# Unread TensorE products at seven value sums of an attention kernel with a feed-forward block

## The chip, the cores and the metric

The kernel runs on one core of a Trainium2 chip. The metric is the device time of one execution in microseconds (us). The engines are named as in the profile: PE is TensorE, PEld its weight loads, DVE VectorE, ACT ScalarE, POOL GpSimd, SP SyncE, whose queue issues the DMAs.

## The reference

Inputs q, k, v of shape (8 batches, 8 heads, 576 positions, 64), w_in (512 x 2048) and w_out (2048 x 512), all float32.

```python
scores = scale * np.matmul(q, k.transpose(0, 1, 3, 2))
kth = np.partition(scores, -top_k, axis=-1)[..., -top_k:-top_k + 1]   # top_k = 32
scores = np.where(scores >= kth, scores, -1000000000.0)
attn = np.exp(scores - np.max(scores, axis=-1, keepdims=True))
attn = attn / (np.sum(attn, axis=-1, keepdims=True) + 1e-09)
x = np.matmul(attn, v)            # heads are then set side by side: (4608, 512)
h = x @ w_in
out = (h - np.tanh(h)) @ w_out    # (4608, 512)
```

## The kernel before, in words

The attention is cut into 144 steps. A step is one pair of heads and 128 query rows (or the last 64 rows of two pairs of heads, a "rem" step). Its stages lie in successive iterations of one loop (`run`), so that several steps are under way at once:

- `scores` (L238): PE multiplies q and k into PSUM, ACT copies the result out (L246).
- `search` (L268 to L279): DVE finds the 32nd largest score of each row by rounds of MAX8 and MATCH_REPLACE8.
- `mask` (L295 to L315): POOL makes the threshold `tb`, ACT (L308) and POOL (L311) put everything below it out, POOL writes a check (`bad`, L315).
- `expo` (L331): ACT takes the exponentials, with the sum of each row. POOL adds epsilon to the sums (L341), DVE inverts them (L346), and POOL repeats each inverse 64 times into the tile `rx` (L356, `spread`): the "repeated sums" of the change.
- Turning. The exponentials have to stand with the keys on the partitions. In the steps of batch 0 (`pe` steps, the ones that the change touches) PE does that: `turn_pe` makes nine transposes (L412) into three PSUM tiles `zt` of four, four and one, and ACT copies each out into `et` (L415). In the other steps DVE and DMAs do it (`turn_z`, `spread_keys`).
- `values` (L436, L444, L448, L460): ten PE products (five chunks of keys, two heads) sum the values into `av[:, 0]`, a transpose of `rx` (L444) sets the repeated sums beside them in `av[:, 1]`, ACT copies both out as `xs` (L448), and POOL multiplies the two (L460) into `xT`, the input of the feed-forward block.
- `ffn_h` (L489, with tanh and the difference at L501 to L503) and `ffn_o` (L510, L520) are the feed-forward block, cut into items of 8 matmul calls or of 2 (L510). `deal` places them between the stages, as many as `rate` asks for; they begin after step 3, which ends the first block of 128 rows.

In a `pe` step n the order in which PE's instructions are written is, in iteration n+2: eight transposes (two `zt` tiles), the scores of step n+3, the ninth transpose (the third `zt` tile), feed-forward items if there are any, then `values(n)`. ACT's order in the same iteration is: two copies of `zt` (L415), L308 of the step after, the conversion of the weights (below), the copy of the scores (L246), the third copy of `zt` (L415), the exponentials of the step after (L331), the tanh of an item, and the copy `xs` (L448). Each engine works its own list in order.

`values(n)` is called only for the last step of a group of rows. In batch 0 the first two blocks of 128 rows have groups of one step (steps 0 to 7); then two steps make a group (8 and 9, and so on).

The pool `zt_ps` has two PSUM buffers; `zt` tiles and `av` tiles share the tag "zt" and with it these two buffers. A tile that takes a buffer waits for the last reader of the tile that had it.

In the first some 160 us the weights are also converted (`convert`, L148 to L173): DMAs bring 32 pieces, and DVE, ACT and POOL work on each. The scheduler follows the program order (`manual_schedule`), and the framework sets the waits.

Of the kernel before, what the change touches and what calls it, by code (L numbers as in the profile page):

```python
# [10 lines left out]
FP32 = mybir.dt.float32  # L11
# [37 lines left out]
def kernel(  # L49
# [9 lines left out]
    nc = tc.nc  # L59
    P = nc.NUM_PARTITIONS  # L60
# [22 lines left out]
    def pool(name, bufs, **kw):  # L83
        return ctx.enter_context(tc.tile_pool(name=name, bufs=bufs, **kw))
# [15 lines left out]
    zt_ps = pool("zt_ps", 2, space=PS)  # L100
    h_ps = pool("h_ps", 2, space=PS)

    ident = consts.tile([P, P], FP32, name="ident")
# [80 lines left out]
    def half(t):  # L184
        return slice(t * D, (t + 1) * D)
# [179 lines left out]
    def tiles(x, nq):  # L365

        x = x[:, 0 : nq * 2 * S]
        return x.rearrange("p (a k i j) -> p a k i j", a=NG, k=KC, j=G)
# [28 lines left out]
    def turn_pe(n):  # L397
# [10 lines left out]
        for k0 in range(0, KC, J):  # L408
# [10 lines left out]
            if k0:  # L419
                yield  # L420

    def values(n):

        g = steps[n]
        nq, u = g.nq, g.unit
        et = tiles(ets.pop(n), nq)
        rx = rxs.pop(n)
        w = nq * P
        av = zt_ps.tile([P, 2, N], FP32, tag="zt", name="av")
        for i in range(2 if g.rem else 1):  # L430
            cols = half(i) if g.rem else slice(0, w)
            es = et[:, 2 * i : 2 * i + 2] if g.rem else et
            hp = g.hp + i
            for c in range(J + 1):
                for t in range(2):
                    nc.tensor.matmul(  # L436
                        av[half(t), 0, cols],
                        vb[g.b, hp][:, t, c, :] if c < J else vr[g.b, hp][:, t, :],
                        es[:, :, (J + 1) * t + c if c < J else J].rearrange("p a i j -> p a (i j)"),
                        start=(c == 0),  # L440
                        stop=(c == J),
                    )
        for i in range(nq):
            nc.tensor.transpose(  # L444
                av[:, 1, 0:w].rearrange("p (a i j) -> p i a j", a=NG, i=nq)[:, i], rx[:, i].rearrange("p t d -> p (t d)"), ident[:]
            )
        xs = xrpool.tile([P, 2, N], FP32, tag="xs", name="xs")
        nc.scalar.copy(xs[:, :, 0:w], av[:, :, 0:w])  # L448
        if g.rem:
            for i in range(2):  # L450
                nc.gpsimd.tensor_tensor(
                    xt(u)[:, g.hp + i, g.col : g.col + R],
                    xs[:, 0, half(i)],
                    xs[:, 1, half(i)],
                    ALU.mult,
                )
        else:

            xv = xs[:, :, 0:w].rearrange("p s (a i j) -> p s i a j", a=NG, i=nq)
            nc.gpsimd.tensor_tensor(  # L460
                xt(u)[:, g.hp, g.col : g.col + w].rearrange("p (i a j) -> p i a j", a=NG, i=nq),
                xv[:, 0],
                xv[:, 1],
                ALU.mult,
            )
        if n in done:
            work.extend(ffn(u))
# [3 lines left out]
    def xt(u):  # L471
        if u.xT is None:
            p = xpool if u.tag == "xT" else xrpool
            u.xT = p.tile([P, CD, N], FP32, tag=u.tag, name=u.tag)
        return u.xT
# [48 lines left out]
    def ffn(u):  # L524

        nh = CF * u.n // (2 * P)
        for item in range(nh):
            f = (item + 1) * CF // nh - 1
            yield CD * (f // FJ + 1), u, lambda item=item: ffn_h(u, item)
        for i in range(len(u.blocks)):  # L530
            for part in range(CF // 2):
                yield CD * (WJ + part // 2 + 1), None, lambda i=i, part=part: ffn_o(u, i, part)

    steps, done, work = [], {}, []

    def plan():
        steps.clear(), done.clear()

        def block(b, qt):
            return [(slice(0, P), out[b * S + qt * P : b * S + (qt + 1) * P, :])]

        rest = None
        for b in range(B):
            if b % 2 == 0:
                rest = Unit(
                    [[(half(i), out[(b + i) * S + JP : (b + i + 1) * S, :]) for i in range(2)]], "xTr"
                )

            parts = [(0, 1), (2, 3)]
            if b == 0:
                parts[0:1] = [(0,), (1,)]
            for a, qts in enumerate(parts):
                unit = Unit([block(b, qt) for qt in qts], "xT")
                pe = b == 0
                for hp in range(NHP):
                    for i, qt in enumerate(qts):
                        steps.append(Step(b, hp, qt, unit, 0, i, len(qts), pe))
                    if hp == NHP - 1:  # L560
                        done[len(steps) - 1] = unit
                    if hp % 2 and a == (0 if b == B - 1 else len(parts) - 1):
                        steps.append(Step(b, hp - 1, J, rest, b % 2 * R, pe=pe))
                        if hp == NHP - 1 and b % 2:
                            done[len(steps) - 1] = rest
        for g, after in zip(steps, steps[1:]):
            if after.pe and not after.rem and not g.pe:
                g.lag = 3
# [4 lines left out]
    def run(exact):  # L573
# [119 lines left out]
        for n in range(-4, NS + 4):  # L693
# [3 lines left out]
            for m in (n - 4, n - 3):  # L697
                if 0 <= m < NS and steps[m].last and steps[m].lag == n - m:
                    values(m)
# [22 lines left out]
            if pe and steps[n - 2].last:  # L722
                values(n - 2)
# [52 lines left out]
```

## Time and profile before

| what | value |
|---|---|
| median of 4 runs | 1539.3 us (1537.58 to 1540.37) |
| profiled execution | 1538.49 us, its span 1536.7 us |
| PE busy | 1439.6 us, 94% of the span |
| PEld busy | 910.0 us, 59% |
| DVE busy | 1347.0 us, 88% |
| POOL busy | 940.9 us, 61% |
| ACT busy | 883.4 us, 57% |
| mean granted clock of PE | 0.98 |

The span goes from the first to the last instruction that the profiler records; the time of the execution is 1.8 us longer. The granted clock is the share of full speed that PE was given in a stretch of time. Busy shares are means over the whole span; the early part, in which the weights are converted, looks different from the rest. In a list of instructions in order of time each line gives the start, the duration, the engine, the line of the kernel, the operation, the tiles (out<-in), the shape, the number of records, and in brackets how long the engine was idle before it and what ended that. One float32 matmul call leaves two MATMUL records, a transpose one.

### The profile page before, as it was taken

The page shows a single profiled execution, that of the slowest core. Times are in us where ns is not written, and L with a number is a line of the kernel's source. Part 1 is how long each engine was busy: PE and PEld are TensorE (multiplying, and loading weights), DVE is VectorE, ACT ScalarE, POOL GpSimd, SP SyncE. Part 2 cuts the span into 40 slices and gives each one's busy share as a digit, 9 for nine tenths or more (in the row PEclk, how much of TensorE's full clock was granted, in tenths as well). Part 3 has the DMA queues.
Part 4 walks back from the last instruction along what each step waited for, and adds up shares of the span by engine and source line. Part 5 has one row for each costly group of instructions (what it writes and reads, how often), then busy time and mean ns, then how long its engine had stood idle before and what let it go on. Part 6 is the DMA issues. An engine that isn't in the chain of part 4 may idle for free.

```text
span 1536.7 us, 24174 instructions
## 1 busy us (share of the span) xinstructions
PE 1439.6 (94%) x7428; PEld 910.0 (59%) x7428; DVE 1347.0 (88%) x3828; ACT 883.4 (57%) x1567; POOL 940.9 (61%) x1525
## 2 busy tenths in 40 slices
PE   2567898999999999999999999999999999999997
PEld 1355566565666666656566665656566665656673
DVE  7997999999999999999999999999999999997300
ACT  4887776566555555555555565556565565655320
POOL 3777576567666665656575675757575675746420
PEclk9787999999999999999999999999999999999999
DMA  9954214547755575446754575446655566534400
GB/s 250 363 182 146 50 32 108 138 142 175 183 142 145 139 174 155 130 138 153 184 139 138 146 172 159 128 141 155 177 136 147 145 154 164 146 115 116 138 7 16
DMA packets 255466, 221.61 MB, mean 144 GB/s; under 512 B 197728, under 2 KB 204896, under 8 KB 248160
## 3 DMA queue, kind: packets, MB, share of 16 engines
q1 hardware_dynamic: 253552, 219.75, 53.0%
q8 instruction: 61, 1.00, 0.3%
q14 instruction: 77, 0.63, 0.1%
q10 hardware_dynamic: 1776, 0.22, 0.1%
HBM read 136.17 MB, written 83.76 MB: 143 GB/s over the span
## 4 chain that ended last, share of the span: by engine, by line
PE 77%; DVE 9%; ACT 4%; DMA 4%; POOL 2%; SPq 2%; issue 2%; DVEq 0%; ACTq 0%; POOLq 0%
PE hps L489 30%; PE ops L510 27%; PE av L436 10%; PE scps L238 9%; DVE m L276 2%; DVE ab L279 2%; PE av L444 2%; SPq L201 1%; DMA et<-there 1%; DMA zx<-in_moe_w_in_dram 1%; ACT z L308 1%; PE zt L412 1%; POOL z L311 1%; DMA there<-spare 1%; DVE ab L268 1%
## 5 line engine op out<-in xcount | busy, mean ns | idle before, releaser
L510 PE MATMUL ops<-w_out,g 128*128 128x512 f32 x1152 | 520.3, 598 | 0.0
L276 DVE MAX8 m<-ab 128x8 f32<-128x288 f32 (+1 forms) x1152 | 471.5, 457 | 0.0
L489 PE MATMUL hps<-xT,w_in 128*128 128x256 f32 (+1 forms) x2176 | 470.1, 371 | 1.2 <-POOL xT L460 1.2
L311 POOL TENSOR_TENSOR z<-sc,z 128x576 f32<-128x576 f32 x288 | 400.2, 1411 | 75.3 <-ACT z L308 75.3
L489 PEld LDWEIGHTS hps<-xT,w_in 128*128 128x128 f32 x2176 | 389.6, 192 | 73.9 <-issue 21.8
L279 DVE MATCH_REPLACE8 ab<-m,ab 128x288 f32<-128x288 f32 x864 | 381.5, 456 | 0.0
L510 PEld LDWEIGHTS ops<-w_out,g 128*128 128x128 f32 x1152 | 211.3, 191 | 244.6 <-issue 240.5
L308 ACT ACTIVATE z<-sc,tb 128x576 f32<-128x576 f32 x288 | 207.6, 769 | 153.4 <-POOL tb L295 153.4
L503 POOL TENSOR_TENSOR g<-g,th 128x512 f32<-128x512 f32 x144 | 183.7, 1276 | 123.4 <-ACT g L502 106.6
L331 ACT ACTIVATE z<-z,nb 128x576 f32<-128x576 f32 x288 | 221.6, 773 | 8.8 <-POOL z L311 8.7
L246 ACT COPY sc<-scps 128x1152 f32<-128x1152 f32 x144 | 160.8, 1117 | 108.8 <-PE scps L238 106.6
L238 PE MATMUL scps<-kT,qT 64*128 64x288 f32 (+1 forms) x1280 | 188.1, 445 | 29.7 <-DVE qT L223 27.3
L238 PEld LDWEIGHTS scps<-kT,qT 64*128 64x128 f32 (+1 forms) x1280 | 101.5, 184 | 118.5 <-issue 55.9
L436 PE MATMUL av<-et,vb 128*64 128x256 f32 (+1 forms) x1088 | 132.9, 380 | 39.0 <-ACT et L415 31.4
L268 DVE TENSOR_TENSOR ab<-scps,sc 128x576 f32<-128x576 f32 x144 | 108.9, 757 | 68.0 <-POOL bad L315 56.2
L460 POOL TENSOR_TENSOR xT<-xs 128x256 f32<-128x256 f32 (+1 forms) x68 | 47.3, 695 | 167.8 <-ACT xs L448 167.8
L501 ACT ACTIVATE th<-hps 128x512 f32<-128x512 f32 x144 | 85.4, 593 | 106.8 <-PE hps L489 104.4
L448 ACT COPY xs<-av 128x512 f32<-128x512 f32 (+1 forms) x84 | 44.1, 525 | 169.4 <-PE av L444 169.4
L436 PEld LDWEIGHTS av<-et,vb 128*64 128x64 f32 x1088 | 74.8, 139 | 101.2 <-issue 35.9
L341 POOL TENSOR_SCALAR rd<-den 128x2 f32<-128x2 f32 x144 | 33.4, 232 | 139.4 <-ACT z L331 91.4
L271 DVE MAX8 ab<-ab 128x8 f32<-128x288 f32 x288 | 117.9, 456 | 0.0
L269 DVE TENSOR_TENSOR ab<-scps,sc 128x576 f32<-128x576 f32 x144 | 108.9, 756 | 0.0
(67 smaller groups left out, 1264.9 us busy)
## 6 DMA issues: line engine op xcount, KB each, us to landing
et<-there SPq DMA_DIRECT2D x224, 288.0 KB, 5.1
there<-spare SPq DMA_DIRECT2D x28, 1152.0 KB, 4.2
there<-zx SPq DMA_DIRECT2D x28, 1152.0 KB, 4.2
kin<-in_k_dram SPq DMA_DIRECT2D x116, 72.0 KB, 2.4
vb<-in_v_dram SPq DMA_DIRECT2D x64, 128.0 KB, 4.4
out_dram<-ot SPq DMA_DIRECT2D x32, 256.0 KB, 3.5
qin<-in_q_dram SPq DMA_DIRECT2D x113, 72.0 KB, 3.3
spare<-there SPq DMA_DIRECT2D x56, 144.0 KB, 3.1
```

Of the source, the lines that this page charges most:

```text
L238: nc.tensor.matmul(ps[rows, t, s, 0:S2], qT[g.b, g.hp + i][half(t), qs], kT[g.b, g.hp + i][half(t), ks], start=True, stop=True,)
L246: nc.scalar.copy(sc[:], ps[:, :, :, 0:S2])
L268: nc.vector.tensor_tensor(lo, ps[:, :, 0, 0:S2], sc[:, :, 1, :], ALU.min)
L276: nc.vector.max(m[:, t, m8], last[t] if i == rounds - 1 else cur[t])
L279: nc.vector.match_replace(nxt[t], m[:, t, m8], cur[t], NEG)
L308: nc.scalar.activation(zv[:, t, :], scf[:, t, :], AF.Relu, bias=tb[:, t : t + 1], scale=-BIG)
L311: nc.gpsimd.tensor_tensor(zv[:, t, :], scf[:, t, :], zv[:, t, :], ALU.subtract)
L331: nc.scalar.activation(x["zv"][:, t, :], x["zv"][:, t, :], AF.Exp, bias=x["nb"][:, t : t + 1], scale=scale, accum_out=den[:, t : t + 1],)
L436: nc.tensor.matmul(av[half(t), 0, cols], vb[g.b, hp][:, t, c, :] if c < J else vr[g.b, hp][:, t, :], es[:, :, (J + 1) * t + c if c < J els ...
L489: nc.tensor.matmul(cur[u][:, s : s + w], w_in[j][:, c, fo : fo + P], u.xT[:, c, 0:w], start=(c == 0), stop=(c == CD - 1),)
L503: nc.gpsimd.tensor_tensor(g, g, th[:], ALU.subtract)
L510: nc.tensor.matmul(cur[u][:], u.g[o // 1024][:, o % 1024 // 512, o % 512 : o % 512 + P], w_out[f // FJ][:, f % FJ, :], start=(f == 0), sto ...
```

## The change

For the steps n of the range 2 to 10 for which `values(n)` is called, that is 2, 3, 4, 5, 6, 7 and 9, `values` gets two groups of products whose results nobody reads: identity times identity, 128x128 float32. Six calls stand ahead of the ten value products. They write to a `zt` tile of their own ("idle"), which is allocated just before `av`. Three more calls stand between the value products and the transposes of the repeated sums; they write to the first 128 columns of `av[:, 1]`, which these transposes then overwrite.

```diff
+    def warm(x, k):
+
+        for _ in range(k):
+            nc.tensor.matmul(x, ident[:], ident[:], start=True, stop=True)
+
     def values(n):
...
         w = nq * P
+        cold = n in thin
+        if cold:
+            warm(zt_ps.tile([P, 512], FP32, tag="zt", name="idle")[:, 0:P], FILL[0])
         av = zt_ps.tile([P, 2, N], FP32, tag="zt", name="av")
...
                         start=(c == 0),
                         stop=(c == J),
                     )
+        if cold:
+            warm(av[:, 1, 0:P], FILL[1])
         for i in range(nq):
...
     steps, done, work = [], {}, []
+
+    thin = range(2, 11)
+    FILL = 6, 3
```

## The prediction

> **What bounds the kernel now.** I read the page first (busy tenths and granted clock), then the same window by window, then TensorE's and ScalarE's instructions in order of time, the waits, and the chain. From the page, two of its rows of 40 slices of 38.4 us:
>
> ```profile
> PE  2567898999999999999999999999999999999997
> PEclk9787999999999999999999999999999999999999
> ```
>
> From about 180 us to the end PE is full at full clock; PE and DVE set the time there, and nothing is changed there. The change works before that, where PE has holes and the clock is below full. Most of what delays that early stretch delays the end one for one: the chain that ended last runs from 160 to 200 us through PE, ACT, POOL and DVE without a rest, and DVE is then busy 20.00 of each 20 us.
>
> The early holes are the steps whose values the change touches. It names steps 2 to 10, but `values` runs only for the last step of a pair: 2, 3, 4, 5, 6, 7 and 9. One of them, step 2, on PE and then on ACT (start, duration, what, in brackets idle before and what ended it):
>
> ```profile
> 66.86 1.09 PE L436 MATMUL av<-et,vb 128*64 128x128 f32 x14
> 74.30 0.48 PE L436 MATMUL av<-et,vb 128*64 128x128 f32 x1 [6.34 <-ACT et L415]
> ...
> 75.54 0.47 PE L444 MATMUL av<-ident,rx 128*128 128x128 f32 x1
> 75.81 1.92 PE L412 MATMUL zt<-ident,z 128*128 128x128 f32 x8
> ```
>
> ```profile
> 73.98 0.26 ACT L415 COPY et<-zt 128x128 f32<-128x128 f32 x1
> ...
> 76.05 0.37 ACT L448 COPY xs<-av 128x256 f32<-128x256 f32 x1 [0.28 <-PE av L444]
> 76.96 0.58 ACT L415 COPY et<-zt 128x512 f32<-128x512 f32 x1 [0.54 <-PE zt L412]
> 77.76 0.58 ACT L415 COPY et<-zt 128x512 f32<-128x512 f32 x1 [0.21 <-PE zt L412]
> 78.24 1.44 ACT L308 ACTIVATE z<-sc,tb 128x576 f32<-128x576 f32 x2
> ```
>
> See three things. ACT is the step's bound: from 77.76 to the next xs copy at 88.22 it works without a gap, and per step it idles only some 1.0 us (0.28+0.54+0.21), all of it for PE. PE waits long for ACT's *third* et copy, but 14 of the 20 value products are done before that wait (they need only the first two copies); only 6 stand behind it. And what follows the wait runs at half clock: eight transposes take 1.92 us, against 1.04 at 103.16. So at most PE's slowness costs ACT about 1 us a step here.
>
> The clock, PE's busy time in stretches of 3.4 us (columns: stretch, length, PE busy, clock, DMA):
>
> ```profile
> 68.93:72.34 3.41, 0.00 (x0) 1.00 0.53 172
> 72.35:75.75 3.40, 1.33 (x7) 0.50 0.91 337
> 75.76:79.16 3.40, 3.40 (x15) 0.50 0.98 389
> 79.17:82.58 3.41, 1.73 (x19) 1.00 0.07 26
> ...
> 123.55:126.95 3.40, 1.38 (x19) 1.00 0.96 319
> 126.97:130.36 3.39, 2.14 (x11) 0.50 1.03 327
> ```
>
> The clock changes on fixed edges 3.41 us apart. A stretch 1.73 busy is followed by full clock, one 1.38 busy or less by half clock; from half it comes back only after a full stretch (3.40), not after 2.14.
>
> **The change, part by part.** *Price of one product.* A call of a float32 matmul leaves two records (L489: 8 calls of an item, 16 records). Sixteen records of 128x128 at full clock run from 101.37 to 103.16, 0.112 us each; at half clock from 129.53 to 132.94, 0.213. So six calls (12 records) cost 1.34 or 2.56 us, three calls (6) 0.67 or 1.28. The 20 value records of 256 columns take 2.31 us at full clock in the chain; at 128 columns that is 1.15 at full, 2.31 at half.
>
> *The extra tile.* This is the part I think decides. Tiles of the tag zt share two PSUM buffers in turn: zt, zt, zt, av in each step, so av has taken the buffer of the step's *second* zt tile. The trace shows that: at 174.33 the fifth transpose of a step (its second zt tile) waits 0.24 for the xs copy, the reader of the av before it; the first four don't. Now the idle tile takes that buffer, and av takes the *third* zt tile's, whose reader is the et copy at 73.98. Then all 20 value records wait for that copy, where 6 did: at E, the moment the wait ends (74.30 in step 2), 2.31 us of half-clock work stand before the sum's transpose, not 1.12, and the three calls add 1.28.
>
> *When the L444 transpose starts.* Now at E+2.31+1.28 = E+3.59 at half clock, E+1.15+0.67 = E+1.82 at full, and never before POOL's rx. Before: E+1.24 and +1.14 in steps 2 and 3, E+2.47, 2.38, 2.35, 2.35 in steps 4 to 7 (101.20, 115.52, 129.26, 146.67 less 98.73, 113.14, 126.91, 144.32). In steps 4 to 7 POOL's rx ends last, so full-clock products hide there and half-clock ones cost 1.1 to 1.2. No DMA and no instruction of another engine is added. Behind L444 on PE stand the next zt transposes, the scores and the feed-forward items; ACT's xs copy waits for it, and behind that its whole queue.
>
> *What the six calls do for the clock.* They run right after the third zt transpose, so they lie at the start of the hole, not its end. In step 2 they end at 66.86+1.34 = 68.2 and PE then waits until 74.30; the stretch 68.93 to 72.34 stays empty, and E is at half clock as before. Same in step 3. So, with the edges where they lie in this execution, by steps (z is ACT's start of L308, the mark of a step's lateness):
> - Step 2: L444 at 77.89, 2.35 late; clock back at 79.17, so five of the eight transposes are slow; the et copies start 2.4 and 2.1 late, z **+2.15**.
> - Step 3: E at 88.7, half clock until 92.83, L444 at 92.3; the transposes are then nearly all fast, z at 94.4 against 90.41, so **+1.85** more.
> - Step 4: E at 102.7. PE is through the transposes at 93.6, and 1.24 of scores, one transpose and 3.67 of feed-forward items later at 98.75; the fill ends at 100.1, and the stretch from 99.65 is busy some 0.85: half clock from 103.07. L444 0.7 late, the first items behind it slow: **+0.9**.
> - Step 5: the hole of 2.6 us is split by an edge; both stretches are over 2 us busy, full clock. L444 follows rx; z is held by POOL's tb (it waited 0.26 for it), so faster transposes bring only **-0.1**.
> - Step 6: in step 5 transposes and scores ran fast (1.04 and 1.24 us, before 1.92 and 2.29), so PE comes to the wait earlier and the hole is 3.7 us; half clock at E, L444 +1.24, but of the 16 items behind it (3.41 slow before) half run fast: **-0.1**.
> - Step 7: the hole stays over 3.4 us, half clock, **+1.2**.
> - Step 9: nothing waits. PE is on the chain, and the 18 records add 1.34+0.67 = **+2.05**:
>
> ```profile
> 170.98 2.31 PE av L436 x20
> ...
> 173.69 0.59 ACT xs L448
> ...
> 179.74 0.76 DVE ab L268
> ```
>
> Here PE's lateness reaches DVE at 179.74, which idled 2.39 before. Sum: 2.15+1.85+0.9-0.1-0.1+1.2+2.05 = 7.95 us. The profiled execution took 1538.5 (span 1536.7, 1.8 around it): 1546.5. The median shown is 0.8 higher, 1539.3, so 1547.
>
> *Bounds.* All seven at half clock without recovery: 2.35+2.45+(1.12+1.6)+1.2+1.2+1.2+2.05 = 13.2, 1552.5. Full clock throughout: steps 2 and 3 lose 0.6 to 0.7 at L444 and win as much in the transposes; 4 nothing; 5 -0.1; 6 -1.8 (16 items 1.62 faster, and transposes); 7 -0.8; 9 +2.05: -0.65 in all, and -2.7 if step 9's is hidden. I take the middle because the rows give both clocks in turn.
>
> A rule that would speak for the change: the Trainium skill, "TensorE: Matmul & The Clock Gate", "Why this matters for your kernels", asks for no idle gaps over some 3 us between bursts. The trace differs: PE's gap before 126.91 is only 2.02 us, and half clock follows, as its stretch was 1.38 of 3.40 busy. By the page's rule the 2.6 us hole of step 4 would keep full clock and the sum would be an estimated 7.05 us (7.95 less step 4's 0.9); by the rows it is 7.95.
>
> **Rivals.** *The clock stays up, and the products pay for themselves.* The six calls lift each hole's stretches over the 1.73 that kept full clock, so L444 still follows rx in steps 4 to 7. For it: step 6's stretch missed by 0.35 us. Against: in steps 2, 3 and 7 the hole is far longer than the fill. It decides when E falls at full clock in at least steps 4, 6 and 7; the time is then 1538.5-0.65, about 1538 (1539 by the median): not slower. *The sums keep their early start, and the clock stays up.* If av doesn't wait for the third copy, in steps 2 and 3 four slots and three calls (0.45+0.67) hide under rx, and each step wins 0.8; with 5 to 7 (-0.1-1.8-0.8) -4.3, if step 9's products are hidden too: 1535. Against: the turn of two buffers, and step 9 on the chain. *The unread products are dropped,* or hide wholly: 1539.
>
> **How the numbers follow.** Forecast, slower by 3 to 13 us: 0.70. Clock stays up: 0.17; dropped: 0.03. Early start and clock: 0.10. A measurement can tell about 0.2%, 3.1 us: faster 0.10, same 0.20, slower 0.70. The range goes from 1537, into the second case, to 1552.5, the upper bound.
>
> **What would show it.** PE's value group behind the wait has 20 records in steps 2 to 7, none before it; L444 starts some 3.5 us after E in steps 2 and 3; ACT's idle time before xs there grows from 0.2-0.3 to over 2 us; half clock still stands at 74 and 86 us; DVE L268 of 179.74 comes some 8 us later. Wrong if 14 records still run early, or if the clock stays at 1.00 from 90 us on.

## The result, and the profile after

The changed kernel takes 1542.5 us (median of 42 executions), before 1539.5 (median of 63): ratio 1.0019, 95% interval 1.0015 to 1.0024. It is 3.0 us slower. The forecast had the direction, with 1547, some 8 us over before; the change cost less than half of these 8 us.

The page of the changed kernel, the same two rows in 40 slices as shown for before:

```profile
PE   2588798999999999999999999999999999999997
...
PEclk9789999999999999999999999999999999999999
```

PE is fuller in the third and fourth slice (8 and 8, before 6 and 7) and a tenth emptier in the fifth, and the granted clock has 9 in the fourth where it had 7; in the third it stays at 8. So the products run where they were meant to, and the clock is higher in part of that stretch. Step 2 again, on PE (the products are line L425, the value products now L444, the transpose of the repeated sums L454):

```profile
68.36 1.82 PE L425 MATMUL idle<-ident 128*128 128x128 f32 x12
70.24 1.09 PE L444 MATMUL av<-et,vb 128*64 128x128 f32 x14
74.78 0.32 PE L444 MATMUL av<-et,vb 128*64 128x128 f32 x1 [3.46 <-ACT et L415]
...
75.36 1.25 PE L425 MATMUL av<-ident 128*128 128x128 f32 x6
76.40 0.42 PE L454 MATMUL av<-ident,rx 128*128 128x128 f32 x1
76.61 1.92 PE L412 MATMUL zt<-ident,z 128*128 128x128 f32 x8
```

Fourteen value records still run ahead of the wait for ACT's third copy, six behind it. That is the line on which the prediction broke: it had all 20 behind the wait, and named 14 early records as a sign that it was wrong. The six early calls have shortened the hole from 6.34 to 3.46 us, and the wait ends at full clock (records of 0.32 us, before 0.48). But the three late calls then put the L454 transpose 1.62 us behind the end of the wait, before 1.24, and the eight transposes still take 1.92. PE's busy time and clock in stretches of 3.4 us show why (columns: stretch, length, PE busy, clock, DMA):

```profile
69.19:72.59 3.40, 2.08 (x23) 1.00 0.57 169
72.60:76.00 3.40, 1.22 (x11) 0.98 0.93 348
76.02:79.41 3.39, 3.39 (x16) 0.52 0.85 321
```

The stretch that held the rest of the hole was 1.22 us busy, and half clock followed it. Before, half clock held for two stretches, 72.35 to 79.16, over value products and transposes; now it holds for one, which begins one stretch later and still has the transposes in it. The fill shortened the dip, as such a time at half clock is called here, and did not remove it. What the three late calls do is plain on ACT, in steps 2 and 3:

```profile
76.86 0.37 ACT L458 COPY xs<-av 128x256 f32<-128x256 f32 x1 [0.60 <-PE av L454]
...
90.32 0.37 ACT L458 COPY xs<-av 128x256 f32<-128x256 f32 x1 [1.48 <-PE av L454]
```

The xs copies of these two steps waited 0.28 and 0.19 us before.

Where the time came from is read by taking the same instruction in the two traces. I take the first value record behind the wait in each step (in step 9 the first transpose, then DVE's L268). The traces start 0.47 us apart; "change" is the step's own part.

| instruction | before, us | after, us | later by | change |
|---|---|---|---|---|
| step 2, value record | 74.30 | 74.78 | 0.48 | |
| step 3 | 86.56 | 87.38 | 0.82 | step 2: 0.34 |
| step 4 | 98.73 | 100.84 | 2.11 | step 3: 1.29 |
| step 5 | 113.14 | 116.71 | 3.57 | step 4: 1.46 |
| step 6 | 126.91 | 130.47 | 3.56 | step 5: 0 |
| step 7 | 144.32 | 146.62 | 2.30 | step 6: -1.26 |
| step 9, first transpose | 162.55 | 164.95 | 2.40 | steps 7, 8: 0.10 |
| DVE L268 behind step 9 | 179.74 | 183.09 | 3.35 | step 9: 0.95 |

The sum is 2.9 us, the size of the median's 3.0. But not every step's part comes from the change. The kernel e8_only9 below has the products in step 9 alone, so its steps 2 to 7 are those of before, and its first value records behind the wait in steps 4, 5, 6 and 7 are these:

```profile
99.04 0.32 PE L444 MATMUL av<-et,vb 128*64 128x128 f32 x1 [1.97 <-ACT et L415]
115.07 0.32 PE L444 MATMUL av<-et,vb 128*64 128x128 f32 x1 [2.93 <-ACT et L415]
128.84 0.32 PE L444 MATMUL av<-et,vb 128*64 128x128 f32 x1 [1.77 <-ACT et L415]
144.49 0.48 PE L444 MATMUL av<-et,vb 128*64 128x128 f32 x1 [4.41 <-ACT et L415]
```

Against before they are later by 0.31, 1.93, 1.93 and 0.17: step 4 costs 1.62 and step 6 wins 1.76 with no product added there. So the 1.46 and the -1.26 of the table are of the size that one execution differs from another by. Steps 2 and 3 of e8_only9 show no such difference (0.00 and 0.01); the parts of these two steps and of step 9 are the ones to hold the change to.

This profiled execution itself took 1545.5, 3 above its median; some 2.7 us of that came at one place far from the change (columns: stretch, length, busy of PE, PEld, DVE, ACT, POOL, clock, DMA):

```profile
403.50:406.90 3.40, 1.33 (x7) 0.49 (x7) 3.40 (x14) 0.70 (x3) 0.52 (x2) 1.00 1.00 181
407.00:410.40 3.40, 3.40 (x19) 2.13 (x14) 3.40 (x9) 0.00 (x0) 0.00 (x0) 0.51 0.47 164
```

A stretch with only 1.33 us of PE work was followed by one at half clock. The gap ahead of the value products there was 1.0 us longer than before (2.07 for 1.10), and the products themselves took 1.7 more, 3.99 us to the transposes for 2.31. Of the thirteen traces this one alone has the dip at 407 us, and only it and that of before have one near 270 us. The edges of the stretches, too, lie at another place in most of the traces; that this decides which dips come is not shown. The 42 executions span 6.7 us, the 63 of before 6.1. Single traces are therefore read here step by step, and verdicts come from medians.

### The profile page after: what moved, and what is told of

It is laid out like the page before. It is cut to its first block, busy times and chain, and to the rows that moved or that the text cites. A ratio compares the mean times of both kernels' runs of the same rounds, so it can differ in the third digit from the quotient of the medians.

```text
span 1543.7 us, 24420 instructions
## 1 busy us (share of the span) xinstructions
PE 1452.5 (94%) x7554; PEld 924.3 (60%) x7554; DVE 1347.6 (87%) x3828; ACT 883.4 (57%) x1567; POOL 942.9 (61%) x1525
## 4 chain that ended last, share of the span: by engine, by line
PE 77%; DVE 9%; ACT 4%; DMA 3%; POOL 2%; SPq 2%; issue 2%; DVEq 0%; ACTq 0%; POOLq 0%
PE hps L499 30%; PE ops L520 27%; PE av L444 10%; PE scps L238 9%; DVE m L276 2%; DVE ab L279 2%; PE av L454 2%; SPq L201 1%; DMA zx<-in_moe_w_in_dram 1%; DMA et<-there 1%; ACT z L308 1%; POOL z L311 1%; DMA spare<-in_moe_w_out_dram 1%; DVE ab L268 1%; DVE ab L269 1%
## 5 line engine op out<-in xcount | busy, mean ns | idle before, releaser
L268 DVE TENSOR_TENSOR ab<-scps,sc 128x576 f32<-128x576 f32 x144 | 108.5, 754 | 70.7 <-POOL bad L315 59.3
L444 PE MATMUL av<-et,vb 128*64 128x256 f32 (+1 forms) x1088 | 133.4, 382 | 34.1 <-ACT et L415 25.1
L444 PEld LDWEIGHTS av<-et,vb 128*64 128x64 f32 x1088 | 74.9, 140 | 95.9 <-issue 32.1
```

The lines of the kernel that those rows point to most:

```text
L268: nc.vector.tensor_tensor(lo, ps[:, :, 0, 0:S2], sc[:, :, 1, :], ALU.min)
L444: nc.tensor.matmul(av[half(t), 0, cols], vb[g.b, hp][:, t, c, :] if c < J else vr[g.b, hp][:, t, :], es[:, :, (J + 1) * t + c if c < J els ...
```

## The experiments

Eleven kernels, in three groups; the kernel before was run beside each group, with medians of 1539.2, 1540.8 and 1540.7 us. So each run is compared with the before of its own group.

| run | what is filled (early + late calls) | median, us | before | ratio, 95% interval |
|---|---|---|---|---|
| the change | 6+3 in steps 2 to 7 and 9 | 1542.5 | 1539.5 | 1.0019 (1.0015 to 1.0024) |
| e1_ahead | 6+0 | 1538.7 | 1539.2 | 0.9997 (0.9988 to 1.0006) |
| e2_late | 0+3 | 1540.1 | 1539.2 | 1.0005 (0.9996 to 1.0014) |
| e3_no9 | 6+3, not in step 9 | 1539.3 | 1539.2 | 0.9997 (0.9988 to 1.0006) |
| e4_held | 6+3, idle buffer held | 1547.4 | 1539.2 | 1.0053 (1.0040 to 1.0067) |
| e5_long | 6 to 24 early, not in 9 | 1537.4 | 1540.8 | 0.9979 (0.9970 to 0.9989) |
| e6_ahead_no9 | 6+0, not in 9 | 1538.1 | 1540.8 | 0.9983 (0.9974 to 0.9992) |
| e7_late6 | 0+6 | 1547.0 | 1540.8 | 1.0040 (1.0027 to 1.0053) |
| e8_only9 | 6+3 in step 9 alone | 1542.1 | 1540.8 | 1.0007 (0.9997 to 1.0016) |
| e9_from0 | e5, and 8 and 20 in steps 0, 1 | 1538.3 | 1540.7 | 0.9983 (0.9974 to 0.9992) |
| e10_turn9 | e5, and 22 ahead of step 9's transposes | 1536.5 | 1540.7 | 0.9970 (0.9959 to 0.9981) |
| e11_in_av | e10, written into av | 1538.2 | 1540.7 | 0.9980 (0.9970 to 0.9990) |

**The wait that did not come (e4_held).** The theory after the result: the prediction's price for the wait was right, and only its premise wrong, that av would take the third zt tile's buffer. The rival: the price was wrong as well. Keeping the idle tile in use until after the sums forces av to the other buffer.

```diff
-            warm(zt_ps.tile([P, 512], FP32, tag="zt", name="idle")[:, 0:P], FILL[0])
+            idle = zt_ps.tile([P, 512], FP32, tag="zt", name="idle")[:, 0:P]
+            warm(idle, FILL[0])
...
-            warm(av[:, 1, 0:P], FILL[1])
+            warm(idle, FILL[1])
```

> The nine calls as in the change, but the three late ones write to the idle tile too, so that its buffer is still held when the value tile is allocated, and the value tile has to take the third zt tile's buffer: the wait that the prediction had assumed. If the prediction's price of that wait holds: 14 more records wait for the third copy in each of the seven steps, 1546 to 1548. If the wait is nearly free, because the clock is up when it ends: 1542.5, as the changed kernel.

Measured: 1547.4, 8.2 us over before. Its PE in step 2 (lines one further on):

```profile
67.06 1.50 PE L425 MATMUL idle<-ident 128*128 128x128 f32 x12
74.64 1.97 PE L445 MATMUL av<-et,vb 128*64 128x128 f32 x16 [6.07 <-ACT et L415]
76.40 0.64 PE L445 MATMUL av<-et,vr 128*64 128x128 f32 x4
76.97 1.65 PE L425 MATMUL idle<-ident 128*128 128x128 f32 x6
78.41 0.42 PE L455 MATMUL av<-ident,rx 128*128 128x128 f32 x1
```

All 20 value records stand behind the wait, at half clock, and the transpose comes 3.77 us behind its end (forecast 3.59). From the same instructions as in the table above, the steps 2, 3, 4, 5, 6, 7 with 8, and 9 cost 2.13, 1.97, 1.09, 0, -0.55, 1.09 and 2.50, 8.2 us in all; the prediction had 2.15, 1.85, 0.9, -0.1, -0.1, 1.2 and 2.05. The price holds; the premise did not.

**Early or late calls (e1_ahead, e2_late, e7_late6).** Theory A: the late calls are the cost. Theory B: the early ones are.

```diff
-    FILL = 6, 3
+    FILL = 6, 0    # e1_ahead; e2_late has 0, 3 and e7_late6 has 0, 6
```

> Only the six early calls, the three late ones taken out. Theory A (the three late calls stand on the path of the xs copy in steps 2, 3 and 9; the six early ones pay back, or cost nothing, by keeping the clock): the changed kernel's lateness against before, 0.33 in step 2, 1.29 in step 3 and 0.67 of step 9's products, goes, 2.3 us: about 1540.2, 0.7 us over before. Theory B (the six early calls cost the time, and the late ones hide under POOL's repeated sums): 1542.5, as the changed kernel.

> Only the three late calls, the six early ones taken out. Theory A: the late calls cost 2.3 us (0.33+1.29+0.67) and what the early ones won in step 6 (1.25 us) is gone: 1541.8 to 1543.5. Theory B: 1539.5, as before.

> Only late calls, six in place of three. Theory A (they stand on the path to the xs copy): steps 2 and 3 pay 1.28 more each, steps 4 to 7 come out from behind the repeated sums by up to 1.3 at half clock, step 9 0.67 more: 4 to 8 us over the run with three, 1544 to 1548. Theory D (the three late calls' cost is chance, of the place of the clock's edges): 1540 as with three.

Without the late calls nothing is lost (0.5 us under before, within the interval), so theory B falls. Six late calls cost 6.2 us, as theory A had it. Three of them alone cost 0.9 us, with an interval of -0.6 to 2.2: less than theory A's 2.3 to 4.0 over the 1539.5 that it started from, a miss in size. The trace of e2_late shows the path that A means:

```profile
75.63 1.65 PE L425 MATMUL av<-ident 128*128 128x128 f32 x6
77.07 0.42 PE L454 MATMUL av<-ident,rx 128*128 128x128 f32 x1
```

They run at half clock, 1.44 us from their start to the transpose's. That execution is 3.1 us late by DVE's L268 behind step 9 (steps 2, 3 and 4 some 0.95 each), and wins 1.4 back at about 270 us, where the profiled execution of before has a dip and this one none. Early and late alone add to 0.4 us, both together to 3.0; the intervals of the two runs, some 1.4 us each way, leave room for most of that, but whether the two groups also hurt each other stays open.

**Step 9 (e3_no9, e8_only9).**

```diff
-    thin = range(2, 11)
+    thin = range(2, 9)     # e3_no9; e8_only9 has range(9, 10)
```

> Both groups, but not in step 9, where PE waits for nothing. Theory A: step 9's 18 records cost between the 0.95 us that the trace of the changed kernel shows there and their full 2.05 us; without them 1540.4 to 1541.5. Theory B (the lateness of step 9 is taken up before DVE's next search): 1542.5.

> Both groups in step 9 alone. Theory A, by the prediction's working: PE is on the chain there and the 18 records add 2.05 us: 1541.2. If part is taken up elsewhere, as the trace of the changed kernel has it: 0.95, 1540.1. If step 9 costs nothing: 1539.2.

Without step 9 the time is that of before, 3 us less than the change, more than A's 1 to 2; step 9 alone costs 1.3 (interval -0.5 to 2.5). Both agree with the forecast's 2.05 within their intervals. That nothing is lost there is spoken against by e3_no9 alone, as the interval of e8_only9 has room for it. In e3_no9 the steps 2 to 7 with all their products cost nothing that the median shows (interval -1.8 to 0.9), though its trace has 1.20 and 1.05 us in steps 2 and 3; the two runs add to some 1 us and the change costs 3.0, so how the 3.0 divide between step 9 and the others is known only roughly. The chain of waits of the changed kernel has all 18 records on it:

```profile
172.29 1.34 PE idle L425 x12
173.62 2.31 PE av L444 x20
175.93 0.86 PE av L425 x6
...
183.09 0.76 DVE ab L268
```

**Would a fill that fits win? (e5_long, e6_ahead_no9.)** Theory A says that half clock behind the wait costs ACT its time; theory C that POOL holds the steps anyway.

```diff
-    thin = range(2, 11)
-    FILL = 6, 3
+    thin = range(2, 8)
+    FILL = {2: 22, 3: 24, 4: 6, 5: 10, 6: 10, 7: 18}
...
-            warm(zt_ps.tile([P, 512], FP32, tag="zt", name="idle")[:, 0:P], FILL[0])
+            warm(zt_ps.tile([P, 512], FP32, tag="zt", name="idle")[:, 0:P], FILL[n])
...
-            warm(av[:, 1, 0:P], FILL[1])
+            warm(av[:, 1, 0:P], 0)
```

In e5_long the early calls number `FILL[n]`; e6_ahead_no9 has 6 and 0 with steps 2 to 8.

> Only early calls, not in step 9, and as many as fill most of each hole: 22, 24, 6, 10, 10 and 18 calls in steps 2 to 7, at 0.224 us each at full clock. Theory A (half clock behind the wait is what costs ACT its 1 us a step): the granted clock is full at the end of the wait, the eight transposes take 1.04 us and not 1.92, and the time falls by up to 0.8+0.8+0.1+1.8+0.8 = 4.3 us, to 1535 to 1537. Theory C (the clock brings nothing, since POOL's repeated sums and threshold hold the steps): 1539. If the calls run at half clock and overrun the wait: 1541 or more.

> Six early calls in steps 2 to 7 only, no late ones. Theory A: the run with early calls alone (1538.7) still paid step 9's 1.34 us; without it 1537.3. Theory C: 1539, as before.

e5_long is 3.5 us faster than before, e6_ahead_no9 2.7. Both clear of before, and not of each other. Step 2 in e5_long, and among its waits the one on POOL (in total, times, longest):

```profile
67.10 5.08 PE L425 MATMUL idle<-ident 128*128 128x128 f32 x44
72.23 1.09 PE L444 MATMUL av<-et,vb 128*64 128x128 f32 x14
73.66 0.32 PE L444 MATMUL av<-et,vb 128*64 128x128 f32 x1 [0.34 <-ACT et L415]
...
74.90 0.33 PE L454 MATMUL av<-ident,rx 128*128 128x128 f32 x1 [0.59 <-POOL rx L356]
75.07 1.28 PE L412 MATMUL zt<-ident,z 128*128 128x128 f32 x8
```

```profile
PE av L454 <- POOL rx L356: 8.0, 6, 1.7
```

The hole is down to 0.34 us, the clock is full at the end of the wait, and the transposes take 1.28. Step 2 is as theory A has it. What is late next is theory C's: the L454 transpose waits for POOL's repeated sums in six steps, 8.0 us in total, which bounds what a higher clock can bring. And behind that wait half clock can come back, as in step 3:

```profile
87.09 0.33 PE L454 MATMUL av<-ident,rx 128*128 128x128 f32 x1 [1.23 <-POOL rx L356]
87.25 1.84 PE L412 MATMUL zt<-ident,z 128*128 128x128 f32 x8
```

In step 7 the transposes take 1.91, also as before. So the medians show that both kernels win, but not that a full clock in the filled steps is what wins it. By DVE's L268 behind step 9 the trace of e5_long is only 0.8 us further ahead of before than it was ahead of its first extra product, and another 1.4 us comes near 270 us, where before has its dip. e6_ahead_no9, whose six calls fill only a part of the long holes, can't be told from it. Where the 3 us come from stays open. In step 7 of e5_long av went to the third zt tile's buffer after all:

```profile
143.30 1.09 PE L444 MATMUL av<-et,vb 128*64 128x128 f32 x16 [1.41 <-ACT et L415]
```

**Further holes (e9_from0, e10_turn9, e11_in_av).** e9_from0 fills steps 0 and 1 too, e10_turn9 the hole ahead of step 9's transposes, and e11_in_av also writes the early calls into av itself, allocated ahead of them.

```diff
-            warm(zt_ps.tile([P, 512], FP32, tag="zt", name="idle")[:, 0:P], FILL[n])
         av = zt_ps.tile([P, 2, N], FP32, tag="zt", name="av")
+            warm(av[:, 1, 0:P], FILL[n])                     # e11_in_av
...
+        if n == 9:                                           # e10_turn9, in turn_pe
+            warm(zt_ps.tile([P, 512], FP32, tag="zt", name="idle")[:, 0:P], 22)
```

> As the run with long early fills (22, 24, 6, 10, 10, 18 calls in steps 2 to 7), with 8 calls in step 0 and 20 in step 1 as well. Theory A (the transposes behind the wait at full clock win up to 0.8 us a step): 0.5 to 1.6 us below the run with long fills, some 4 to 5 us below before. Theory C (in these two steps the weights' DMAs set the pace, as the chain of before has them between 53 and 60 us): nothing, some 3 us below before.

> As the run with long early fills, and 22 calls more ahead of step 9's transposes, where PE of before waits 6.10 us for ACT and then runs at half clock on the chain. Theory A: transposes 1.04 for 1.97, scores 1.24 for 2.20 and output items 3.60 for 4.14 on the chain: up to 2.4 us below the run with long fills, 5 to 6 us below before. If ACT or POOL ends last there: the same as the run with long fills, 3 below before.

> As the run before it, but the early calls write into the value tile itself, which is allocated ahead of them, so that no idle tile can push it to the third zt tile's buffer; with long fills step 7's value tile had been moved there and its 20 records waited. Theory A: that wait's price in step 7 goes, 0.6 to 1.2 us below the run with the idle tile. If the wait costs nothing at full clock: the same.

They are 2.4, 4.2 and 2.5 us faster than before; with intervals of some 1.5 us each way none can be told from e5_long. Theory A's further gains did not show. In e11_in_av 14 value records of step 7 run ahead of the wait again (from 144.90, the six others from 146.39), and no gain from that can be seen in the time. In e10_turn9 the profiled execution still had 2.60 us of the hole left behind its fill, and step 9's transposes at half clock, 1.97 us. So e10_turn9, with 1536.5 us, has the lowest median of five kernels that beat both; e6_ahead_no9 is the simplest of the five.

## Why the prediction was wrong, point by point

- *What bounds the kernel early on:* right. ACT's wait for PE is what moved in steps 2 and 3 (0.28 to 0.60, 0.19 to 1.48), and the lateness reached DVE's L268 behind step 9 (2.9 us) and the end (3.0 by the medians); the single trace has further differences behind that, such as the dip at 407 us.
- *Price of a product:* right. Twelve early records took 1.44 us from their start at 172.12 to the next product at 173.56 (forecast 1.34), six late ones at half clock 1.44 from 131.51 to the transpose at 132.95 (forecast 1.28).
- *The extra tile:* wrong, and this is the step that failed. I read from two tiles in turn that av would be pushed to the third zt tile's buffer. The idle tile had no use after its last call, and av followed it into the same buffer, the second zt tile's: the 14 records kept their early start, and the fifth transpose behind step 9 still waits 0.24 us for the xs copy, at 177.69. Why the framework chose this buffer here and the other in step 7 of e5_long is not shown. e4_held puts the assumed wait in and gives 1547.4, the forecast; the step's price is therefore 5 us, the distance between e4_held and the change as ratios have it (1.0053 less 1.0019, 0.0034 of 1539).
- *The clock in the holes:* half right. Half clock stayed in steps 2 and 3, but fell on the transposes in one and on value records, calls and transposes in the other; in steps 5 to 7 the wait ended twice at full clock (steps 5 and 7, records of 0.32 us), as the fill lay in the same stretch as the value records. Step 6 won 1.26 where I had 0.1, and step 4 lost 1.46 where I had 0.9; as e8_only9 shows the like with no products there, neither speaks for or against the working.
- *The late calls in steps 4 to 7 hide under POOL's repeated sums at full clock:* right. In steps 4 and 5 of the changed kernel L454 still waited 0.83 and 0.85 us for them.
- *Step 9, 2.05:* right within what the runs tell. The two groups of products took 2.2 us there (172.12 to 173.56 and 175.86 to 176.64). The trace has 0.95, as the scores and output items ahead of them ran at a higher clock (1.74 and 3.60 us, before 2.20 and 4.14); they come before the products of step 9, so this gain is not theirs, and counts as luck.
- *Rivals:* the one called "early start and the clock stays up" had the right premise and the wrong outcome, because the clock didn't stay up with six calls. With e5_long's calls and none late its outcome, 4.3 us, came within 0.8; the trace does not show that it came the way the rival says.

A rule that speaks against such a reading of the clock: the Trainium skill, "TensorE: Matmul & The Clock Gate", "Part 4: PE-mode transpose", says beside bfloat16 figures that full clock "doesn't engage" for transposes, which don't count as PE work "the same way". The trace of before, with float32 transposes, differs: of the stretch 62.10 to 65.51, busy 3.35 us, 1.91 us were transposes, and full clock followed at 65.52.

## What to carry to other kernels

Products that nobody reads cost nothing that could be measured when six stood ahead of a wait (e1_ahead). Behind the wait they are on the path, as six there cost 6.2 us (e7_late6), unless something else ends later still, as POOL's repeated sums did in steps 4, 5 and 7. Where there is no wait, as in step 9, they are on the path too. To hold the clock over a hole they have to leave no stretch of it too empty: six calls only shortened the dip of step 2, and 22 in its hole of 6.3 us kept the clock up; but 24 in step 3 did not keep it up behind the next wait, and the longer fills won no more time than six calls that could be told. One step of one trace proves little: a kernel that leaves the step as it was shows how much it differs by itself. A tile added to a shared pool is to be looked up in the finished program or a trace, not counted out by turns, since who waits for whom hangs on it.

## What the runs showed of the hardware that was not expected

The granted clock comes back from half after one full stretch when that stretch follows the fall at once (76.02 to 79.41, 3.39 busy); in step 2 of before it took two, as the first was 1.33 busy. And a single half-clock stretch can be worth more than half of the whole change: the one at 407 us made the value products there 1.7 us longer. In steps whose code was the same, two traces differed by up to 1.8 us a step (before and e8_only9, steps 4 and 6).
